# Reading the moving operand of every float32r product in a turned order: a linear-attention and gated feed-forward block on one core

## The chip, the cores and the metric

The kernel runs on one core of one Trainium2 chip. The metric is the device time of one execution in microseconds; lower is better. The five engines of the core that matter here are TensorE (PE in the profile; its weight loads are listed as PEld), VectorE (DVE), ScalarE (ACT), GpSimd (POOL), and SyncE (SP), whose queue issues all the DMAs.

## The reference

The input x has 2048 tokens of 512 features, all in float32. In short:

```python
xn = layernorm(x)                                   # over the features
q, k, v = split(xn @ wqkv)                          # 32 heads of 16
pq, pk = phi(q), phi(k)                             # phi(t) = (t + 1 if t > 0 else exp(t)) + 1e-6
kv = einsum("bhsd,bhse->bhde", pk, v);  z = pk summed over the tokens
o  = (pq @ kv) / (pq . z + 1e-6)
s  = o @ wo
g  = silu((gelu(xn @ w_gate) * (xn @ w_up)) @ w_down)   # inner width 1792
y  = x + s * g
```

The time of the kernel is mostly that of these matrix products.

## The kernel before, in words

**Products.** Accuracy is kept by splitting each float32 operand into a high and a low float32r part, and a product is made of three float32r matmuls: high by high, high by low, low by high (`three`, L443). The class `Sum` (L418) collects such parts into one PSUM bank; its inner function calls `nc.tensor.matmul(o, a, b)` (L437), where `o` is the output in PSUM, `a` the stationary operand (128 by 128, loaded as weights) and `b` the moving operand, 512 columns wide, and in the last two sums of the kernel 256. All float32r products of the kernel go through L437, but for two in `run_z` (L928). Plain float32 products are left in three places: the warming matmuls (L467), the transposes (L638), and the four small products for kv (L983); none of these is changed.

**Stages.** The program runs in one launch, in this order, with neighbours overlapped:

1. For 16 token tiles: layer norm, transposes, the products for q and k with a Strassen-like scheme of seven half-size products (banks named X, Y, Z, with the tokens as the stationary operand and the weights `kq` as the moving one), and phi. `gacc` adds up the Gram sums `gps` of the k features (moving: `pk`) over the tokens, and POOL adds up `zacc`. The transposed and split x tiles (`Xh`, `Xl`) are kept in SBUF, some are spilled to DRAM.
2. The feed-forward part, in two passes over the tokens (1024 each), each with seven pairs of 128-wide gate and up blocks. In `quad` (L1136), seven products per block go to the banks FX, FY and FZ; here the weights are stationary and x is moving, so the 512 columns of the output are tokens. The results leave PSUM through `esaved` (ACT copies into `fu`), `gelu` (ACT, straight from PSUM or from a sum), and `c_out` (DVE sums and products into `g` and `h`). From `h`, DVE and ACT make the split forms `hfh`, `hfl` (`h_form`, `h_sums`).
3. `down_strassen` (L1095) multiplies the forms of w_down (`dh`, `dl`, stationary) by `hfh`, `hfl` (moving) in the banks dX, dY, dZ and adds the results to the accumulators `acc` on DVE. It is interleaved with stage 2.
4. Attention's end: `pkv`, the matrix M made of it and wo, the normalised q transposed by tiles to DRAM (`turn`, L1218), and the sums `sps` (`attn`, L1260), M stationary and transposed q moving. `out_tile` (L1312) multiplies `sps` by the silu of `acc`, adds a tile of x transposed from DRAM (`sxr`) and writes the transposed output.

**Order.** The whole order of operations is written out in a list of 3626 numbers (`ORDER`, L18); each engine runs its own in that order, with semaphores between engines. So no engine takes work ahead of its turn.

**Host.** `kernel` (L1420) permutes some inputs before the launch: the q columns of wqkv and the features of x are laid out by heads (`order`), and x is given in transposed form too (`A_xT`). The output comes back transposed.

Of the kernel before, what the change touches and what calls it, by code (L numbers as in the profile page):

```python
# [10 lines left out]
AF = mybir.ActivationFunctionType  # L11
# [222 lines left out]
class Plan:  # L234
# [9 lines left out]
    def do(self, eng, cost, fn, out, *ins, more=(), lat=0.0, key=None, name="", kb=0, port=True, sum=None):  # L244


        op = Op()
        op.no, op.table, op.due = len(self.ops), TABLES.get(name), self.due
        op.eng, op.cost, op.lat, op.key, op.name = eng, cost, lat + self.HOP[eng], key, name
        op.fn = lambda: fn(out(), *[i() if isinstance(i, View) else i for i in ins])  # L250
        op.pre, op.suc, op.kb = set(), [], kb
        op.port = eng == "POOL" or eng == "DVE" and port and not any(
            isinstance(v, View) and v.psum for v in (out, *ins))
        outs = set(out.res)
        for m in more:
            outs.update(m.res)
        for i in ins:
            if isinstance(i, View):
                for r in i.res:
                    if r not in outs:  # L260
                        op.pre.update(r.writers)
                        r.readers.append(op)
        for r in outs:
            if sum is None or r.sum is not sum:
                r.before = {*r.writers, *r.readers}
                r.writers, r.readers, r.sum = [], [], sum
            op.pre.update(r.before)
            r.writers.append(op)
        for v in (out, *more, *ins):
            if isinstance(v, View) and v.gen:  # L270
                assert not v.gen.over, name
                if v.gen.prev:
                    op.pre.update(v.gen.prev.ops)
                v.gen.ops.add(op)

        op.banks = [v.gen for v in (out, *more, *ins) if isinstance(v, View) and v.psum and eng != "PE"]
        op.pre.discard(op)
        for p in op.pre:
            p.suc.append(op)
        self.ops.append(op)  # L280
        return op
# [5 lines left out]
def act(n, psum=False):  # L287
    return 0.06 + (0.00083 if psum else 0.00095) * n


def dve(n):
    return 0.065 + 0.00105 * n


def pool(n):
    return 0.18 + 0.0021 * n
# [3 lines left out]
def kernel(  # L300
# [14 lines left out]
    nc = tc.nc  # L315
# [6 lines left out]
    NC = 512  # L322
# [5 lines left out]
    do = plan.do  # L328
# [8 lines left out]
    def tile_in(pool_name, unit, shape, dtype, name, parts=1):  # L337

        gen = gens[pool_name, unit] = Gen(gens.get((pool_name, unit)))
        kept = []  # L340

        def get():
            if not kept:
                kept.append(pools[pool_name].tile(shape, dtype, name=name, tag=f"{pool_name}{unit}", bufs=1))
            return kept[0]
        v = View([Res() for _ in range(parts)], get, gen, pool_name == "ps")
        v.unit = unit
        return v
# [7 lines left out]
    def U(tag, places, name, dtype=F32, shape=(P, D), parts=1):  # L356
        return tile_in("up", ring(tag, places), list(shape), dtype, name, parts)
# [9 lines left out]
    def bank(i, name, shape=(P, D)):  # L367
        return tile_in("ps", i, list(shape), F32, name)
# [33 lines left out]
    def copy(eng, dst, src, n, name=""):  # L402
        if eng == "ACT":
            do("ACT", act(n, src.psum), lambda o, i: nc.scalar.copy(o, i), dst, src, name=name)  # L404
        else:
            do("DVE", dve(n), lambda o, i: nc.vector.tensor_copy(o, i), dst, src, name=name)

    def tt(eng, op, dst, a, b, n, name=""):
        e, c = (nc.vector, dve(n)) if eng == "DVE" else (nc.gpsimd, pool(n))
        do(eng, c, lambda o, p, q: getattr(e, f"tensor_{op}")(o, p, q), dst, a, b, name=name)  # L410
# [4 lines left out]

    subs = {}

    class Sum:  # L418


# [4 lines left out]
        def add(self, key, *parts, name="", cost=PASS):  # L425

            for n, part in enumerate(parts):
                regions = [abr[2] if len(abr) > 2 else None for abr in part]
                for r in regions:
                    self.passes[r] = self.passes.get(r, 0) + 1  # L430

                def run(o, *v, regions=regions):
                    for a, b, r in zip(v[::2], v[1::2], regions):

                        first = not self.on and not self.made
                        made = self.made[r] = self.made.get(r, 0) + 1
                        nc.tensor.matmul(o if r is None else o[:, r], a, b, start=first, stop=made == self.passes[r],  # L437
                                         skip_group_check=self.on or r is not None)
                do("PE", cost * len(part), run, self.ps, *[v for abr in part for v in abr[:2]],
                   key=(*key, "part", n), name=name, sum=self)  # L440
                subs.setdefault(key, []).append((*key, "part", n))
# [342 lines left out]
    for n in range(NP):  # L784
# [6 lines left out]
        for i in range(2):  # L791
# [6 lines left out]
            if n < CL:  # L798
                if i:
                    b = tile_in("up", 19 + n, [P, 2, 2, P], F32R, f"b12_{n}", 2)  # L800
# [113 lines left out]
    for c in range(KT):  # L914
        g = U("p", range(24, 28), f"GT{c}")
# [9 lines left out]

    def run_z(o, a, *zs):
        for n, z in enumerate(zs):
            nc.tensor.matmul(o, a, z, start=n == 0, stop=n == 1)  # L928
    do("PE", 2 * PASS, run_z, pz, ones_r, *zs, key="z")
    zq = const("zq", [P, P])  # L930

# [59 lines left out]
    for g in range(KT):  # L991
        v = tile_in("dp", 1 + g, [P, 2, D], F32R, f"wos{g}", 2)
        wos.append([v.part(v.res[hl:hl + 1], (slice(None), hl)) for hl in range(2)])
        split(*wos[g], wo_sb[g], D, "wo")
    for g in range(KT):
        pm = bank([6, 7, 5, 6][g], f"pm{g}")
        Sum(pm).add(("m", g), *three([[v[:, g] for v in kvs]], [wos[g]]), name="m")
        m = [tile_in("up", 19 + 2 * g + hl if g < 2 else 25 + 2 * g + hl, [P, D], F32R, f"m{hl}{g}") for hl in range(2)]
# [71 lines left out]
            for k in range(n):  # L1070
                ds[u, slots[k]] = [v[:, k] for v in f]

    def gelu(v, src, q, key):
        do("ACT", act(NC), lambda o, i: nc.scalar.activation(o, i, AF.Gelu_apprx_tanh), v, src, name="gelu")
        gs[key] = v

    hf, hforms = {}, {}
# [1 line left out]
    def h_form(u, slot, src):  # L1079
        f = hforms[u, slot] = U("hh", FHH, f"hfh{slot}_{u}", F32R), U("hl", FHL, f"hfl{slot}_{u}", F32R)  # L1080
        split(*f, src, NC, "h")

    def h_sums(p, u):
        def t():
            i = ring("hsum", range(3))
            return spare(p).part(spare(p).res[4 + i:5 + i], (slice(None), 2 + i))
        h = {key: hf.pop((u, key)) for key in (11, 12, 21, 22)}
        t1, t2, t3, t4 = t(), t(), t(), t()
        for slot, o, a, b in ((3, t1, h[12], h[11]), (4, t2, h[22], t1), (5, t3, h[22], h[12]), (6, t4, h[21], t2)):
            tt("DVE", "sub", o, a, b, NC, "T")  # L1090
            h_form(u, slot, o)
# [44 lines left out]
    def quad(q, p):  # L1136
        u, is_up = divmod(q % NQ, 2)

        def esaved(ps, name):
            e = U("fe", FE, name)  # L1140
            copy("ACT", e, ps, NC, name)
            return e

        def c_out(key, e, ps):

            if not is_up:
                g = U("fg", FG, f"g{key}_{q}")
                if e is None:
                    gelu(g, ps, q, (u, key))
                else:  # L1150
                    tt("DVE", "add", g, e, ps, NC, "c")
                    gelu(g, g, q, (u, key))
                return
            h = U("fc", [*FC, FX[0]], f"h{key}_{q}")
            g = gs.pop((u, key))
            if e is None:
                tt("DVE", "mul", h, g, ps, NC, "h")
            else:
                tt("DVE", "add", h, e, ps, NC, "c")
                do("POOL", pool(NC), lambda o, i: nc.gpsimd.tensor_mul(o, o, i), h, g, name="h")  # L1160
            hf[u, key] = h
            slot = {11: 0, 21: 1, 22: 2}.get(key)
            if slot is not None:
                h_form(u, slot, h)
            if key == 12:
                h_sums(p, u)

        X, Y, Z = bank(q % 2, f"FX{q}"), bank(2, f"FY{q}"), bank(3 + q % 2, f"FZ{q}")
        fprod(X, q, 1, True)
        copy("ACT", Y, X, NC, "seed")  # L1170
        fprod(Y, q, 2, False)
        c_out(11, None, Y)
        fprod(X, q, 6, False)
        u2 = esaved(X, f"fu2_{q}")
        fprod(Z, q, 5, True)
        fprod(X, q, 7, False)
        u3 = esaved(X, f"fu3_{q}")
        c_out(22, u3, Z)
        fprod(X, q, 4, False)
        c_out(21, None, X)  # L1180
        fprod(Z, q, 3, False)
        c_out(12, u2, Z)
# [204 lines left out]
    for c in range(2):  # L1387
        for n in range(KT):
            g = acc[1, 4 * c + n]
# [3 lines left out]
    for s in (0, 1, 4, 3, 5, 6, 2):  # L1393
        for hl in "hl":
            src = View([x_d[hl](j, ()).res[0] for j in range(4)], x_d[hl](0, (slice(None), slice(2 * s, 2 * s + 2))).get)
# [50 lines left out]
```

## Time and profile before

| What | Value |
|---|---|
| Time, median of 3 runs | 597.34 us (595.75 to 598.02) |
| Span of the profiled execution | 594.4 us; its time beside the span is not listed apart |
| TensorE busy, instructions | 586.5 us (99%), 2630 matmuls |
| VectorE busy | 485.8 us (82%), 774 |
| ScalarE busy | 360.1 us (61%), 668 |
| GpSimd busy | 242.7 us (41%), 237 |
| Moved by DMA | 141.29 MB, mean 238 GB/s |

In the rows that follow, a group is given as line, engine, operation, output and inputs by the program's names, partitions by elements, the count, and after the bar the busy time in us, the mean length of one in ns, and the idle time of that engine just before, with what ended it. Rows of a timeline begin with the start in us from the span's beginning and the length in us; where several like instructions follow each other they are merged, with their number at the end. A row of waits gives the waiting engine, the one waited for, and three numbers: us in total, times, longest. A matmul's record is longer than its share of the array, since matmuls overlap, so a rate is read from starts, not from lengths.

### The profile page before, as it was taken

The numbers are of one execution on the slowest core, as the hardware profiler recorded it, in microseconds if no ns is written. First come the engines' busy times: TensorE is split into PE (matmuls) and PEld (weight loads), VectorE is DVE, ScalarE is ACT, GpSimd is POOL, SyncE is SP. The second block draws the span as 40 slices with busy tenths as digits, with TensorE's granted clock in tenths as the row PEclk, the third lists the DMA queues.
The fourth block names the chain that finished last, engine by engine and source line by source line (L and its number), as shares of the span: only waits on it lengthen the run. The fifth ranks groups of instructions, "written<-read, shape, count | busy, mean of one in ns | idle before, by whom it ended". The sixth has DMA issues, their size and how long they took to land.

```text
span 594.4 us, 7882 instructions
## 1 busy us (share of the span) xinstructions
PE 586.5 (99%) x2630; PEld 485.4 (82%) x2630; DVE 485.8 (82%) x774; ACT 360.1 (61%) x668; POOL 242.7 (41%) x237
## 2 busy tenths in 40 slices
PE   9999999999999999999999999999999999999995
PEld 8888888888888888888888887888888888888875
DVE  7999988985887988899988764738787989788896
ACT  5788888877767856555446357856464436355810
POOL 4456776636646482734053822430302130126100
PEclk9999999999999999999999999999999999999998
DMA  7049987678864772736868989965575565638796
GB/s 252 32 146 289 281 254 227 203 254 312 311 219 179 261 290 82 291 133 236 298 252 263 366 322 351 370 254 178 182 243 175 189 239 177 212 124 283 242 288 249
DMA packets 78953, 141.29 MB, mean 238 GB/s; under 512 B 4673, under 2 KB 47681, under 8 KB 74945
## 3 DMA queue, kind: packets, MB, share of 16 engines
q1 hardware_dynamic: 78912, 140.79, 68.8%
q8 instruction: 21, 0.34, 0.2%
q14 instruction: 20, 0.16, 0.1%
HBM read 87.82 MB, written 52.95 MB: 237 GB/s over the span
## 4 chain that ended last, share of the span: by engine, by line
PE 93%; DMA 3%; DVE 2%; SPq 1%; issue 0%; DVEq 0%
PE FX L437 25%; PE FZ L437 13%; PE dX L437 12%; PE gps L437 7%; PE FY L437 6%; PE dY L437 6%; PE X L437 6%; PE sps L437 5%; PE dZ L437 3%; PE Z L437 3%; PE k L437 2%; PE q L437 2%; PE Y L437 1%; DMA Xl<-xl_d 1%; DMA sxr<-in_A_xT 1%; PE warm L467 1%
## 5 line engine op out<-in xcount | busy, mean ns | idle before, releaser
L437 PE MATMUL FX<-Xh,w 128*128 128x512 f32 x448 | 131.7, 390 | 0.0
L437 PEld LDWEIGHTS FX<-Xh,w 128*128 128x128 f32 x448 | 83.9, 188 | 17.7 <-ACT fu L404 0.4
L1160 POOL TENSOR_TENSOR h<-h,g 128x512 f32<-128x512 f32 x28 | 39.2, 1400 | 77.1 <-DVE h L410 39.7
L437 PE MATMUL FX<-Xl,w 128*128 128x512 f32 x224 | 68.3, 389 | 0.0
L437 PE MATMUL FZ<-Xh,w 128*128 128x512 f32 x224 | 68.2, 389 | 0.0
L410 POOL TENSOR_TENSOR sums<-draw 128x256 f32<-128x256 f32 x28 | 25.1, 897 | 96.1 <-DMA draw<-in_B_w_down 74.6
L404 ACT COPY dY<-dX 128x512 f32<-128x512 f32 x56 | 32.1, 574 | 48.6 <-PE dX L437 38.8
L404 ACT COPY fu<-FX 128x512 f32<-128x512 f32 x56 | 32.9, 588 | 47.2 <-PE FX L437 44.1
L437 PEld LDWEIGHTS FX<-Xl,w 128*128 128x128 f32 x224 | 42.0, 188 | 8.8
L437 PEld LDWEIGHTS FZ<-Xh,w 128*128 128x128 f32 x224 | 42.0, 188 | 8.7
L410 POOL TENSOR_TENSOR tmp<-raw 128x256 f32<-128x256 f32 x28 | 25.3, 907 | 48.5 <-DVE w L410 33.6
L1114 DVE TENSOR_TENSOR acc<-acc,dY 128x512 f32<-128x512 f32 x48 | 32.7, 682 | 15.1 <-PE dY L437 14.8
L1114 DVE TENSOR_TENSOR acc<-acc,dX 128x512 f32<-128x512 f32 x48 | 32.8, 683 | 14.1 <-PE dX L437 14.1
L437 PE MATMUL dX<-hfh,dh 128*128 128x512 f32 x112 | 43.4, 390 | 0.0
L404 ACT CAST hfh<-sums 128x512 fp32r<-128x512 f32 x56 | 34.2, 621 | 14.5 <-DVE sums L410 14.1
L437 PE MATMUL dX<-hfl,dh 128*128 128x512 f32 x112 | 42.6, 389 | 0.0
L437 PE MATMUL dX<-hfh,dl 128*128 128x512 f32 x112 | 42.4, 390 | 0.1
L410 DVE TENSOR_TENSOR hfl<-sums,hfh 128x512 fp32r<-128x512 f32 x56 | 40.0, 717 | 1.2 <-ACT hfh L404 0.9
L410 DVE TENSOR_TENSOR hfl<-h,hfh 128x512 fp32r<-128x512 f32 x42 | 32.7, 783 | 3.3 <-ACT hfh L404 2.3
L437 PE MATMUL FZ<-Xl,w 128*128 128x512 f32 x112 | 34.2, 391 | 0.6 <-DMA Xl<-xl_d 0.6
L437 PE MATMUL FY<-Xh,w 128*128 128x512 f32 x112 | 33.8, 389 | 0.0
L717 POOL TENSOR_TENSOR zacc<-zacc,kp 128x512 f32<-128x512 f32 x16 | 24.6, 1538 | 18.9 <-DVE kp L706 18.9
(222 smaller groups left out, 1513.1 us busy)
## 6 DMA issues: line engine op xcount, KB each, us to landing
w<-w_d SPq DMA_DIRECT2D x17, 1792.0 KB, 8.3
w_d<-w SPq DMA_DIRECT2D x11, 1792.0 KB, 7.4
draw<-in_B_w_down SPq DMA_DIRECT2D x14, 512.0 KB, 4.2
w_d<-we SPq DMA_DIRECT2D x18, 256.0 KB, 2.5
x<-in_A_x SPq DMA_DIRECT2D x16, 256.0 KB, 3.1
q_d<-qp SPq DMA_DIRECT2D x16, 256.0 KB, 3.1
qz<-q_d SPq DMA_DIRECT2D x16, 256.0 KB, 4.2
q<-q_d SPq DMA_DIRECT2D x16, 256.0 KB, 3.0
```

Of the source, the lines that this page charges most:

```text
L404: do("ACT", act(n, src.psum), lambda o, i: nc.scalar.copy(o, i), dst, src, name=name)
L410: do(eng, c, lambda o, p, q: getattr(e, f"tensor_{op}")(o, p, q), dst, a, b, name=name)
L437: nc.tensor.matmul(o if r is None else o[:, r], a, b, start=first, stop=made == self.passes[r], skip_group_check=self.on or r is not None)
L467: nc.tensor.matmul(o, w, w, start=True, stop=True)
L717: do("POOL", pool(D), lambda o, i: nc.gpsimd.tensor_add(o, o, i), zacc, p0, name="zacc")
L1114: do("DVE", dve(D), lambda o, i: nc.vector.tensor_add(o, o, i), o, ps, name="acc")
L1160: do("POOL", pool(NC), lambda o, i: nc.gpsimd.tensor_mul(o, o, i), h, g, name="h")
```

## The change

Each float32r product reads its moving operand's columns in a turned order. In every eight columns 0 to 7 the order is 0, 4, 1, 5, 2, 6, 3, 7, so that a read alternates between the first four and the last four. The output's columns come out in that order. The stationary operand, the widths, the number of products, `ORDER` and the DMAs stay.

The rest of the change undoes or carries that order:

- In stage 1 the columns are features of q and k; the columns of wqkv are permuted on the host with the inverse (for k twice, since k's features pass through a second turned product in `gacc` and in the z product). wo is permuted by the inverse once.
- In stage 2 the columns are tokens. `esaved`, `gelu` and `c_out` read PSUM through a view that steps (0, 2, 4, 6, 1, 3, 5, 7 in each eight) and so write SBUF in the natural order.
- In stages 3 and 4 the tokens come out turned once on both sides (`acc` and `sps`); x transposed is turned on the host to match, and the host turns the output back.

```diff
+    def turned(ap):
+        return ap.rearrange("p (o i m) -> p o m i", i=2, m=4)
+    def back(v):
+        return v.map(lambda ap: ap.rearrange("p (o m i) -> p o i m", i=2, m=4))
+    def eights(v):
+        return v.map(lambda ap: ap.rearrange("p (o i m) -> p o i m", i=2, m=4))
...
-                        nc.tensor.matmul(o if r is None else o[:, r], a, b, start=first, stop=made == self.passes[r],
+                        nc.tensor.matmul(o if r is None else o[:, r], a, turned(b), start=first, stop=made == self.passes[r],
...
-            nc.tensor.matmul(o, a, z, start=n == 0, stop=n == 1)
+            nc.tensor.matmul(o, a, turned(z), start=n == 0, stop=n == 1)
...
-    def gelu(v, src, q, key):
-        do("ACT", act(NC), lambda o, i: nc.scalar.activation(o, i, AF.Gelu_apprx_tanh), v, src, name="gelu")
+    def gelu(v, src, q, key, to=None):
+        do("ACT", act(NC), lambda o, i: nc.scalar.activation(o, i, AF.Gelu_apprx_tanh), to or v, src, name="gelu")
...
-            copy("ACT", e, ps, NC, name)
+            copy("ACT", eights(e), back(ps), NC, name)
...
-                    gelu(g, ps, q, (u, key))
+                    gelu(g, back(ps), q, (u, key), eights(g))
...
-                    tt("DVE", "add", g, e, ps, NC, "c")
+                    tt("DVE", "add", eights(g), eights(e), back(ps), NC, "c")
...
-                tt("DVE", "mul", h, g, ps, NC, "h")
+                tt("DVE", "mul", eights(h), eights(g), back(ps), NC, "h")
...
-                tt("DVE", "add", h, e, ps, NC, "c")
+                tt("DVE", "add", eights(h), eights(e), back(ps), NC, "c")
...
+    eights = _np.arange(8).reshape(2, 4).T.ravel()
+    def turned(n):
+        return (_np.arange(0, n, 8)[:, None] + eights).ravel()
+    def back(n):
+        return _np.argsort(turned(n))
-    laid["A_xT"] = _np.ascontiguousarray(laid["A_x"].T)
+    laid["A_xT"] = _np.ascontiguousarray(laid["A_x"].T[:, turned(shape[-2])])
...
-    laid["A_wqkv"] = _np.concatenate([w[:, :d][:, order], w[:, d:2 * d], w[order, 2 * d:]], 1)
+    laid["A_wqkv"] = _np.concatenate([w[:, :d][:, order[back(d)]], w[:, d:2 * d][:, back(d)[back(d)]], w[order, 2 * d:]], 1)
+    laid["A_wo"] = _np.ascontiguousarray(laid["A_wo"][:, back(d)])
...
-    return _np.ascontiguousarray(r.results[0]["out_yT"].T).reshape(shape)
+    return _np.ascontiguousarray(r.results[0]["out_yT"].T[back(shape[-2])]).reshape(shape)
```

## The prediction

> **What bounds the kernel now.** I read the page's busy times first, then the granted clock, the waits of TensorE, the chain that ended last, the starts of single products, and last the busy time by stretches.
>
> ```profile
> span 594.4 us, 7882 instructions
> PE 586.5 (99%) x2630; PEld 485.4 (82%) x2630; DVE 485.8 (82%) x774; ACT 360.1 (61%) x668; POOL 242.7 (41%) x237
> PE 93%; DMA 3%; DVE 2%; SPq 1%; issue 0%; DVEq 0%
> ```
> ```profile
> core 0: 594.4 us, clock 0.997
> ```
> ```profile
> PE warm L467 <- DVE neg_half L459: 1.1, 1, 1.1
> PE FZ L437 <- DMA Xl<-xl_d: 0.6, 1, 0.6
> ```
>
> TensorE is busy for 99% of the span, waits 1.7 us in all for others, and makes 93% of the chain. Its clock is granted nearly in full, so the throttle holds nothing back. The time is therefore the number of products times the time from one start to the next. The busy column can't give that (a product's record is 390 ns long and overlaps the next), so I take starts:
>
> ```profile
> 299.74 0.39 PE L437 MATMUL dY<-hfl,dh 128*128 128x512 f32 x1
> ...
> 303.82 0.39 PE L437 MATMUL dZ<-hfh,dh 128*128 128x512 f32 x1
> ```
> ```profile
> 586.67 0.64 PE L437 MATMUL sps<-pqh,Ml 128*128 128x256 f32 x4
> 587.15 1.12 PE L437 MATMUL sps<-pqh,Mh 128*128 128x256 f32 x8
> ```
> ```profile
> 144.23 2.84 PE L983 MATMUL pkv<-GT,wvo 128*128 128x128 f32 x24
> 146.83 0.70 PE L437 MATMUL FX<-Xh,w 128*128 128x512 f32 x2
> ```
>
> Between the first two rows 18 products of 512 columns start: 4.08 us / 18 = 226.7 ns each. Four products of 256 columns take 0.48 us, 120 ns each. The difference, 106.7 ns for 256 columns, is 0.417 ns a column. Take 512 of those (213.4) from 226.7 and **13.3 ns are left that belong to the product, whatever its width**. The columns themselves already stream at an even rate; the only thing that a better order of reading can win is this remainder, 32 column times per product.
>
> The third pair is the plain float32 product, on the same array and with its own load of weights: 2.60 us / 24 = 108.3 ns for 128 columns. At two column times a column that is 106.7 ns, and 1.6 ns remain. So a load of weights between products doesn't by itself cost 13.3 ns; the remainder goes with float32r, which takes its moving columns twice as fast.
>
> **The change part by part.** *The products.* All float32r products read turned. Their number is the page's 2630 less the plain float32 ones:
>
> ```profile
> L638 PE MATMUL pt<-blk,xn 128*128 128x128 f32 x48 | 7.5, 284 | 0.0
> L467 PE MATMUL warm<-blk 128*128 128x128 f32 x28 | 6.1, 407 | 1.1 <-DVE neg_half L459 1.1
> L983 PE MATMUL pkv<-GT,wvo 128*128 128x128 f32 x32 | 3.9, 275 | 0.0
> L437 PEld LDWEIGHTS FX<-Xh,w 128*128 128x128 f32 x448 | 83.9, 188 | 17.7 <-ACT fu L404 0.4
> ```
>
> 2630 - 48 - 28 - 32 = 2522, and 2522 x 13.3 ns = 33.5 us of remainder in the whole span. No row of this trace has a turned read, so its price has to be bounded. Best end: the remainder goes altogether, -33.5 us. Worst end: a column costs two column times, as in the plain float32 rows, some +0.213 us a product. What I take is a remainder of 1.6 ns, that of the plain float32 row: 11.7 ns x 2522 = **-29.5 us on TensorE**. My reason is what the 32 column times look like. They are the same for 256 and 512 columns, so they follow something that each product has once, and the load of 128 weight columns (188 ns, under way while the product before it streams) is that. Plain float32 has the load too but takes a moving column only every second tick, and pays nearly nothing. So the moving read and the weight read seem to meet when the moving read runs at full rate, one lost tick for four weights. [...] This is a choice between two readings of one number, not a row.
>
> [...]
>
> *The un-turning where TensorE's results leave PSUM in the feed-forward part* (esaved, gelu, the sums and products of c_out). The same instructions, as many elements; PSUM is now read every second column, and SBUF is written in order.
>
> ```profile
> L404 ACT COPY fu<-FX 128x512 f32<-128x512 f32 x56 | 32.9, 588 | 47.2 <-PE FX L437 44.1 <-DVE g L410 2.9
> L410 DVE TENSOR_TENSOR h<-fu,FZ 128x512 f32<-128x512 f32 x28 | 19.1, 682 | 11.1 <-PE FZ L437 10.8 <-ACT fu L404 0.2
> L410 DVE TENSOR_TENSOR g<-fu,FZ 128x512 f32<-128x512 f32 x28 | 19.0, 680 | 9.4 <-PE FZ L437 8.3 <-DMA s_d<-so 1.2
> L1074 ACT ACTIVATE g<-FY 128x512 f32<-128x512 f32 x14 | 8.4, 599 | 1.4 <-PE FY L437 1.4
> L1074 ACT ACTIVATE g<-FX 128x512 f32<-128x512 f32 x14 | 8.3, 596 | 5.4 <-PE FX L437 5.3
> L410 DVE TENSOR_TENSOR h<-g,FX 128x512 f32<-128x512 f32 x14 | 9.5, 680 | 5.5 <-PE FX L437 5.5
> L410 DVE TENSOR_TENSOR h<-g,FY 128x512 f32<-128x512 f32 x14 | 9.5, 678 | 1.0 <-PE FY L437 1.0
> L404 ACT CAST xnh<-xn 128x512 fp32r<-128x512 f32 x16 | 9.9, 624 | 0.9 <-PE gps L437 0.8
> L404 ACT CAST hfh<-h 128x512 fp32r<-128x512 f32 x42 | 25.9, 621 | 6.1 <-POOL h L1160 3.4 <-PE dY L437 2.7
> L612 DVE STREAM_TRANSPOSE sums<-q 128x512 f32<-128x512 f32 x16 | 17.5, 1093 | 0.2
> ```
> ```profile
> L404 ACT COPY fu<-FX x56: 578/587/599, 140.3 to 535.7; 128x512 f32<-128x512 f32 x56
> ```
>
> That is 84 instructions on ACT (56 + 14 + 14) and 84 on DVE (28 + 28 + 14 + 14). Lower end: nothing, as the cast through a permuted view (xnh, runs of 32, most of its 16) takes 624 ns beside 621 in order; a shorter read would end off TensorE's path and gain nothing there. Upper end: the transpose, whose writes step by four elements, 1093 ns, so +0.41 us on each DVE one. I take nothing: xnh is a plain pass with a view, as these are, while the transpose is another operation. The cover is the idle time that the rows show: both engines wait for TensorE before these very instructions (44.1, 10.8, 8.3 us). Were the cover gone at the upper end, the 84 on DVE would add 34.5 us to it over 395 us (140.3 to 535.7), 4.4 us in each 50.
>
> *Layout.* Weights, x transposed and the output are permuted on the host; the same DMAs move the same bytes. The z product's turned read undoes the columns of k. Nothing is added to a queue.
>
> *What is late next.* If TensorE wants 5% less (29.5 of 594.4), the others must keep up in the same order.
>
> ```profile
> 20.00:60.00 40.00, 40.00 (x186) 33.07 (x185) 36.48 (x64) 30.29 (x55) 22.25 (x21) 1.00 0.57 166
> 60.00:100.00 40.00, 40.00 (x185) 32.85 (x184) 36.08 (x65) 32.86 (x62) 28.07 (x26) 1.00 0.83 255
> 250.00:300.00 50.00, 50.00 (x223) 41.39 (x222) 46.37 (x76) 26.67 (x53) 13.32 (x13) 1.00 0.68 239
> 350.00:400.00 50.00, 49.43 (x217) 40.41 (x217) 26.40 (x40) 33.66 (x58) 16.69 (x16) 1.00 0.87 320
> ```
>
> The columns after the length are busy PE, weight loads, DVE, ACT, POOL, then clock, DMA share and GB/s. DVE has 46.37 of 50 in the third row; 50 less 5% is 47.5, so it fits with 1.1 us of air. In the first two it has 72.6 of 80, against 76. In the fourth the x tiles come back from DRAM with the DMA engines at 0.87, and TensorE's one wait for data, 0.6 us, is there. I count the gain of that stretch as lost (50 us x 5% = 2.5), half of the other three's (130 us x 5% / 2 = 3.2), 5.7 in all: an estimate, from those shares.
>
> *The sum:* 594.4 - 29.5 + 5.7 = 570.6 us of span. The median of the three runs, 597.34, is 2.9 above the profiled span, which I keep: **573.5 us**, 4% faster. If nothing is given back and the whole remainder goes, 564; if half the remainder goes, 597.3 - 16.8 + 3 = 584.
>
> **The rivals.** *The order doesn't touch the remainder.* If the 32 column times are a gap between one product's last column and the next one's first, every product keeps 226.7 ns. For it: being independent of the width. Against it: the plain float32 rows, which change weights as often and have 1.6. Time: 597.
>
> *The turned read is slower.* The place is the moving read of every float32r product: in order, four columns lie side by side before the read moves 16 bytes on; turned, every read lands in the other group of four than the last. If the array then takes two column times a column, as it does in the plain float32 rows, 2522 products add up to 0.213 us each, +537: about 1130 us. It decides early: 3 us / 2522 is 1.2 ns a product, three lost column times in 512. Against it stands only that in order the move to the next group, every fourth column, costs nothing that the slope of 0.417 ns shows. [...]
>
> *DVE takes over.* TensorE gets its 29.5 us, but the stepped reads of PSUM cost the 0.41 us above. DVE then needs 46.37 + 4.4 = 50.8 us for what is now the stretch 250 to 300, more than TensorE needs today, and 4.4 more in each of its neighbours. What is left is the gain ahead of 140 us, 140 x 5% = 7 us, and little after it: about 590. For it: DVE is the next engine. Against it: the 624 beside 621.
>
> **How the numbers follow.** About 0.5% (3 us) is what a measurement can tell from no change; the three runs lie within 2.3 us. Chances: remainder mostly or half gone 0.60 (564 to 585); DVE takes over 0.07 (585 to 596, by its size faster for 0.05 and the same for 0.02); order without effect 0.13 (595 to 599); turned read slower 0.20. Hence faster 0.65, same 0.15, slower 0.20. The slow case, with a tail to 1130, is what I leave out: the range is 563 to 600. The likeliest case alone has 564 to 585.
>
> **What the changed profile would show.** Starts of 512 columns 213 to 218 ns apart and of 256 some 108: the step on the products is right; both still 13 ns above the columns: the first rival; a difference of the two above 107 ns: the second. The fu, g and h rows at 588, 597 and 680 ns: the un-turning is free; DVE rows near a microsecond and waits of TensorE for DVE: the third. What is given back shows as waits of TensorE, for DMA near 350 to 400 first. Wrong altogether would make me a granted clock below 0.99, which this trace gives no reason to expect.

## The result, and the profile after

The changed kernel takes 572.08 us (median of 4 runs, 571.42 to 573.22) against 597.1 before: ratio 0.958, 95% interval 0.956 to 0.960. The forecast was 573.5. Its profiled execution took 573.22 us, 1.8 more than its span. From that page and from the answers on clock and waits of the changed kernel:

```profile
span 571.4 us, 7894 instructions
PE 559.5 (98%) x2630; PEld 486.3 (85%) x2630; DVE 486.6 (85%) x774; ACT 358.6 (63%) x668; POOL 242.7 (42%) x237
PE 86%; DMA 5%; DVE 4%; issue 2%; POOL 1%; SPq 0%; ACT 0%; DVEq 0%; POOLq 0%
```
```profile
PE FZ L448 <- DMA Xl<-xl_d: 2.4, 1, 2.4
...
PE dX L448 <- DVE acc L1125: 0.8, 1, 0.8
...
```

The same 2630 matmuls, still bound by TensorE, but no longer by it alone: its share of the chain falls from 93 to 86%, and its waits grow from 1.7 to 4.7 us (beside those shown, the 1.1 at the start as before and two of 0.2, one of them for x from DRAM). The starts of products, from the timeline of the changed kernel:

```profile
279.65 0.59 PE L448 MATMUL FX<-Xl,w 128*128 128x512 f32 x2
...
283.96 0.38 PE L448 MATMUL dX<-hfh,dl 128*128 128x512 f32 x1
```
```profile
562.86 0.61 PE L448 MATMUL sps<-pqh,Ml 128*128 128x256 f32 x4
563.30 1.06 PE L448 MATMUL sps<-pqh,Mh 128*128 128x256 f32 x8
```

Twenty products start in 4.31 us, 215.5 ns each (the long stretch of the first bench below gives 215.8), and those of 256 columns stand 110 ns apart. By the bench's figure 10.9 ns of 226.7 are gone, and 2.4 ns remain beside the 213.4 of the columns. The groups that un-turn:

```profile
L404 ACT COPY fu<-FX 128x512 f32<-128x512 f32 x56 | 32.8, 586 | 39.7 <-PE FX L448 35.4 <-DVE g L410 3.9
L410 DVE TENSOR_TENSOR h<-fu,FZ 128x512 f32<-128x512 f32 x28 | 19.0, 679 | 9.5 <-PE FZ L448 8.9 <-ACT fu L404 0.4
L1085 ACT ACTIVATE g<-FY 128x512 f32<-128x512 f32 x14 | 8.4, 599 | 1.1 <-PE FY L448 1.1
```

586, 679 and 599 ns against 588, 682 and 599: the stepped reads of PSUM cost nothing that these rows show; what shrinks is the wait for TensorE ahead of them.

### The profile page after: what moved, and what is told of

Read it like the earlier page. It is cut to its first block, busy times and chain, and to the rows that moved or that the text cites. A ratio compares the mean times of both kernels' runs of the same rounds, so it can differ in the third digit from the quotient of the medians.

```text
span 571.4 us, 7894 instructions
## 1 busy us (share of the span) xinstructions
PE 559.5 (98%) x2630; PEld 486.3 (85%) x2630; DVE 486.6 (85%) x774; ACT 358.6 (63%) x668; POOL 242.7 (42%) x237
## 4 chain that ended last, share of the span: by engine, by line
PE 86%; DMA 5%; DVE 4%; issue 2%; POOL 1%; SPq 0%; ACT 0%; DVEq 0%; POOLq 0%
PE FX L448 23%; PE FZ L448 12%; PE dX L448 11%; PE gps L448 7%; PE FY L448 6%; PE X L448 5%; PE dY L448 5%; PE dZ L448 3%; PE Z L448 3%; PE sps L448 2%; DMA sxr<-in_A_xT 2%; PE k L448 2%; PE q L448 2%; DMA Xl<-xl_d 2%; DMA g<-g_d 1%
## 5 line engine op out<-in xcount | busy, mean ns | idle before, releaser
L448 PE MATMUL FX<-Xh,w 128*128 128x512 f32 x448 | 127.0, 380 | 0.0
L448 PE MATMUL FX<-Xl,w 128*128 128x512 f32 x224 | 66.1, 379 | 0.2 <-DMA Xl<-xl_d 0.2
L448 PE MATMUL FZ<-Xh,w 128*128 128x512 f32 x224 | 65.9, 379 | 0.0
L448 PE MATMUL FZ<-Xl,w 128*128 128x512 f32 x112 | 33.0, 381 | 2.4 <-DMA Xl<-xl_d 2.4
L966 POOL TENSOR_TENSOR qz<-qz,zq 128x512 f32<-128x512 f32 x16 | 21.7, 1355 | 22.4 <-DMA qz<-q_d 18.5
```

The costliest lines, as they stand in the source:

```text
L448: nc.tensor.matmul(o if r is None else o[:, r], a, turned(b), start=first, stop=made == self.passes[r], skip_group_check=self.on or r is n ...
L966: do("POOL", pool(D), lambda o, z: nc.gpsimd.tensor_mul(o, o, z.unsqueeze(1).to_broadcast([P, KT, P])), rows_of(q), zq, name="u")
```

## The experiments

**Which part of the change does it.** Two kernels split it in two.

`turn_only`, the changed kernel without the un-turning:

```diff
     def back(v):
-        return v.map(lambda ap: ap.rearrange("p (o m i) -> p o i m", i=2, m=4))
+        return v
     def eights(v):
-        return v.map(lambda ap: ap.rearrange("p (o i m) -> p o i m", i=2, m=4))
+        return v
```

> The change without the un-turning in the feed-forward part: all products read turned, but esaved, gelu and c_out read PSUM in order (the feed-forward part's tokens are then in another order than the attention part's, which the kernel does not mend). If the stepped PSUM reads are free, as predicted: within 0.3% of the changed kernel, 571 to 574 us, and the fu, g and h rows at 587, 679, 596 ns in both. If they cost something that the rows hide, such as a later release of a bank: 1 to 3 us less than 572.

Measured: 571.45 us, ratio to before 0.959 (0.957 to 0.961), which overlaps with the changed kernel's.

`unturn_only`, the changed kernel with products in order:

```diff
-  nc.tensor.matmul(o if r is None else o[:, r], a, turned(b), ...
+  nc.tensor.matmul(o if r is None else o[:, r], a, b, ...
...
-  nc.tensor.matmul(o, a, turned(z), start=n == 0, stop=n == 1)
+  nc.tensor.matmul(o, a, z, start=n == 0, stop=n == 1)
```

> The un-turning without the turned products: every product reads in order, esaved, gelu and c_out keep their stepped reads (so the columns are un-turned that were never turned). Theory A and B alike: the whole gain sits in the products, so this runs as the kernel before, 595 to 599 us with starts 226.7 ns apart. If the stepped reads themselves helped or hurt: away from 597 by over 3 us.

Measured: 596.53 us, ratio 1.000 (0.999 to 1.002). The whole gain sits in the order of reading, and the un-turning costs nothing that can be told from noise (the fu, h and g rows of `turn_only`, which reads PSUM in order, have 585, 680 and 599 ns, those of the changed kernel 586, 679 and 599).

**Which orders are fast.** A bench of bare products, one order per stretch of 40.

> Nothing of the block is computed: 16 stretches of 40 products each (128 weight columns, 512 moving columns, back to back, 16 different weight tiles in turn), one order of reading per stretch; read are the starts of the products. Theory A (the moving read at full rate meets the reading of the weights, and an order that alternates between two groups of four columns, 16 bytes each, has room to give way): in order 226.7 ns, turned 215.8, groups of four swapped but read in order (swapped) 226.7, alternating inside a group of four (infour) 226.7, alternating between groups 32 bytes, 64 bytes and 1 KB apart (insixteen, inthirtytwo, infar) 216, four groups in turn (fourlines) 216; bf16 in order 216, since it reads half the bytes. Theory B (the 13 ns are a gap between two products that the turned order happens to shorten, with nothing to do with weights): same for the alternating orders, but bf16 and float32r in order should then differ by no rule, and loading one and the same weight tile every time (oneweight) changes nothing. Theory C (every change of 16-byte group costs): turned would be dearer than in order, which the run of the whole kernel already contradicts; it can still hold for orders that never come back to a group soon (everysecond, everyline: a new group at each of 512 reads): over 226.7, up to 427 ns, where theory A has them at 216 too.

The timeline of this bench; each row is a stretch, and the next start less this one, divided by 40, is the time of one product:

```profile
26.50 9.43 PE L53 MATMUL inorder<-mv,w 128*128 128x512 f32 x40
35.76 8.79 PE L53 MATMUL turned<-mv,w 128*128 128x512 f32 x40
44.39 17.43 PE L53 MATMUL everysecond<-mv,w 128*128 128x512 f32 x40
61.65 9.46 PE L53 MATMUL swapped<-mv,w 128*128 128x512 f32 x40
70.94 13.74 PE L53 MATMUL steptwo<-mv,w 128*128 128x512 f32 x40
84.51 9.45 PE L53 MATMUL infour<-mv,w 128*128 128x512 f32 x40
93.80 8.79 PE L53 MATMUL insixteen<-mv,w 128*128 128x512 f32 x40
102.43 8.80 PE L53 MATMUL inthirtytwo<-mv,w 128*128 128x512 f32 x40
111.06 8.80 PE L53 MATMUL infar<-mv,w 128*128 128x512 f32 x40
119.69 10.90 PE L53 MATMUL fourlines<-mv,w 128*128 128x512 f32 x40
130.43 18.63 PE L53 MATMUL everyline<-mv,w 128*128 128x512 f32 x40
148.88 8.83 PE L53 MATMUL bfloat<-mvb,wb 128*128 128x512 bf16 x40
```

In order 231.5, turned 215.8, alternating 32 bytes, 64 bytes or 1 KB apart (insixteen, inthirtytwo, infar) 215.8 as well. Alternating inside a group of four columns (infour) 232: no gain. Four groups in turn (fourlines) 268, where I had 216; steptwo (0, 2, 4, 6, 1, 3, 5, 7) 339; a new group at each read 431 and 461. So alternating is not what helps by itself, and the orders tried here that leave a group after one column are far dearer (268 to 461). Theory A had 216 for a new group at each read too. The stretch `swapped` is no order of its own: as it is written it reads in order from column four on, and its 232 say no more than that.

In order is 231.5 here and not 226.7. The likely reason is where the four moving tiles lie: in the last bench, with tiles 4096 bytes apart, in order takes 226.8, and in this one, with a single moving tile for all products (`onemoving`, not shown), 227.0. No run varies the addresses alone.

**Whether the weights are to blame.** The prediction's reason was that the moving read collides with the reading of the next product's weights (theory A), an estimate from the 32 column times beside 128 weight columns.

> Nothing of the block is computed: stretches of 40 products, in order and turned, with fewer weight columns, fewer moving columns, and weights spread apart in SBUF. Theory A: what a product costs beside its columns grows with the weights read for it: 128 columns 13.3 ns, 64 columns (halfin) about 7.9, 32 (quarterin) about 5.2, so starts 221 and 218.5 ns apart; turned 215.8 at every width. Narrower moving tiles keep the 13.3: 256 columns 120 ns in order and 109 turned, 128 columns about 67 in order and 56 turned unless the load itself is then the limit. Weights in every second column (bytwo) and every fourth (spreadin): if the collisions count 16-byte groups, the remainder goes to about 24 and 46 ns (237 and 259 ns apart); if they count weights, it stays at 13.3. Theory B (a gap between products): halfin and quarterin stay at 226.7, and the spread weights too. Starting the moving tile two columns off a group of four (shifted) should leave in order at 226.7 by both; turned then crosses groups unevenly and may land between 215.8 and 226.7 by theory A.

The weight loads and the timeline of that bench:

```profile
L53 PEld LDWEIGHTS halfin<-mv,w x40: 134/134/136, 44.4 to 53.4; 128*64 128x64 f32 x40
L53 PEld LDWEIGHTS quarterin<-mv,w x40: 107/108/109, 62.3 to 71.2; 128*32 128x32 f32 x40
```
```profile
44.66 9.36 PE L53 MATMUL halfin<-mv,w 128*64 128x512 f32 x40
53.86 8.80 PE L53 MATMUL halfturned<-mv,w 128*64 128x512 f32 x40
62.49 9.32 PE L53 MATMUL quarterin<-mv,w 128*32 128x512 f32 x40
71.65 8.79 PE L53 MATMUL quarterturned<-mv,w 128*32 128x512 f32 x40
80.28 4.87 PE L53 MATMUL narrowin<-mv,w 128*128 128x256 f32 x40
```

With half the weights a product in order takes 230 ns, with a quarter 229, while the load falls from 188 ns to 134 and 108. Theory A had 221 and 218.5. It falls: the loss doesn't count the weights. One weight tile loaded again and again (`oneweight` of the first bench, not shown) leaves a product at 236.5 ns, no less than the 231.5 of that bench. Turned stays at 215.8 with half and with a quarter of them. Theory B, a gap between two products, had half and quarter unchanged and is not refuted here, but it has no account of why the order should decide.

Three other pairs of this bench are not shown. Weights spread to every fourth column take 240.5 ns in order and 233 turned, but there a load takes 309 to 328 ns, longer than the time from start to start, so this pair may be held by the loads, which no row shows, and says little of the moving read. With the moving tile two columns off a group of four, in order takes 235, where 226.7 was expected, and turned 231.5, so turned loses most of its gain there. Products of only 128 columns take 110.5 ns in order and 111.5 turned, where theory A had 67 and 56: turned products of 256 columns take 111.5 too, so half the columns bring nothing more. 110 to 112 ns is the floor of the float32r stretches in these benches, all with 128 weight columns at these widths; what sets it no run shows.

**A rule for the orders.** What the first bench leaves is theory D, the author's own reading of its times. It goes by the order alone: the columns at its even places are taken as one stream and those at its odd places as another, and what counts is how many reads in a row of a stream lie in one group of four float32r columns (16 bytes). With four in both streams a product took 215.8 ns in that bench (turned, insixteen, inthirtytwo, infar), with two 231.5 and 232 (in order, infour), with one 268 to 461 (fourlines, steptwo, everysecond, everyline). That the array fetches in two streams, as the theory has it, is an estimate from these times; no run shows how the array fetches.

> Nothing of the block is computed: stretches of 40 products, other orders, all tiles at starts of like alignment in SBUF. Theory A (collision with the weights) has fallen in the runs on widths: a quarter of the weights still cost 229 ns in order. Theory D: the columns at even and at odd places of the order are fetched as two streams; a stream keeps full rate when four of its reads in a row lie in one group of 16 bytes, loses 5 to 7% with two, and half or more with one. By D: in order 227 to 232 (two per group in each stream); turned 215.8 also when it starts four columns later, but 227 or more when it starts one column off; each column read twice in a row (doubled: 0,0,1,1,2,2,3,3) 216; pairs read twice (doubledpairs: 0,1,0,1) 216; every second float32r column (stepped: one per group and stream) 340 to 460; bf16 in order 216 (four per stream); every second bf16 column (bfloatstepped: two per stream) 227 to 232; the same turned between two groups (bfloatturned: four per stream) 216. Theory E (float32r is dearer since it needs four bytes a column, and alternating between two groups helps): bfloatstepped and bfloatturned both 216, doubled no better than in order. Width: if the loss is per column, in order 512, 384 and 256 columns lose in proportion (11, 8, 5.5 ns beyond a floor); if per product, 11 each.

```profile
75.28 8.79 PE L55 MATMUL turnedofffour<-mv,w 128*128 128x512 f32 x40
83.92 10.96 PE L55 MATMUL turnedoffone<-mv,w 128*128 128x512 f32 x40
94.71 8.80 PE L55 MATMUL doubled<-mv,w 128*128 128x512 f32 x40
103.34 8.80 PE L55 MATMUL doubledpairs<-mv,w 128*128 128x512 f32 x40
111.98 18.30 PE L55 MATMUL stepped<-mv,w 128*128 128x512 f32 x40
130.10 8.83 PE L55 MATMUL bfloat<-mvb,wb 128*128 128x512 bf16 x39
138.76 9.20 PE L55 MATMUL bfloatstepped<-mvb,wb 128*128 128x512 bf16 x39
147.80 21.87 PE L55 MATMUL bfloatturned<-mvb,wb 128*128 128x512 bf16 x40
168.99 9.88 PE L55 MATMUL last<-mv,w 128*128 128x512 f32 x40
```

The float32r stretches go by D: turned four columns later 216, one column off 270, doubled 216, doubled pairs 216, stepped 453. So does the tile two columns off in the bench before, which leaves each stream two in a row. For bf16 (40 products a stretch, one record missing in two) in order is 216.5 and every second column 226, as D had it and E had not; but bfloatturned takes 530 ns, where both had 216. So D is no rule for stepped bf16 reads; why is open. And its "half or more" for one read in a row is too dear for fourlines of the first bench, 268 ns, where a stream comes back to a group after one other. That can't be the whole reason, since steptwo does so too and takes 339.

The direct test moves one stream against the other:

```diff
+    v = ap.rearrange("p (o i m) -> p o m i", i=2, m=4)
+    steps = [list(s) for s in v.ap]
+    steps[-1][0] = b          # the odd places read b columns behind the even ones; turned is b = 4
```

> Nothing of the block is computed: stretches of 40 products, with all moving tiles at starts of 4096 bytes. First question, per product or per column: in order at 512, 448, 384, 320 and 256 columns beside turned at the same widths. The prediction had 13.3 ns per product at any width; the earlier bench, at other starts, had 14.1, 12.4 and 9.1 ns over turned or its floor for 512, 384, 256. If per column: the loss over turned falls with the width, to half at 256; if per product, it stays. Second, theory D (even and odd places of the order are two streams, each wanting four reads in a row from one group of 16 bytes): the odd places are shifted against the even ones, which keep four per group. Shifted by eight columns (lageight): four per group in both, 215.8. By two or by six (lagtwo, lagsix): two and two in the odd stream, 220 to 232. By one (lagone): three and one, 230 to 270. If instead only the number of groups touched by eight reads counts: lagtwo (groups 0 and 1, as turned) is 215.8, lagsix (groups 0, 1, 2) dearer. Third: a quarter of the weights in order, if the weights have no part at all the same as infull; 229 against 232 before.

```profile
29.44 9.23 PE L60 MATMUL infull<-mv,w 128*128 128x512 f32 x40
38.51 8.27 PE L60 MATMUL infoureight<-mv,w 128*128 128x448 f32 x40
46.61 7.12 PE L60 MATMUL inthreeeight<-mv,w 128*128 128x384 f32 x40
53.57 6.02 PE L60 MATMUL inthreetwenty<-mv,w 128*128 128x320 f32 x40
59.43 4.96 PE L60 MATMUL intwofifty<-mv,w 128*128 128x256 f32 x40
64.22 8.80 PE L60 MATMUL turnfull<-mv,w 128*128 128x512 f32 x40
72.86 7.73 PE L60 MATMUL turnfoureight<-mv,w 128*128 128x448 f32 x40
80.43 5.60 PE L60 MATMUL turnthreetwenty<-mv,w 128*128 128x320 f32 x40
85.86 4.63 PE L60 MATMUL turntwofifty<-mv,w 128*128 128x256 f32 x40
90.33 10.83 PE L60 MATMUL lagone<-mv,w 128*128 128x512 f32 x40
100.99 9.24 PE L60 MATMUL lagtwo<-mv,w 128*128 128x512 f32 x40
110.06 9.23 PE L60 MATMUL lagsix<-mv,w 128*128 128x512 f32 x40
119.12 8.80 PE L60 MATMUL lageight<-mv,w 128*128 128x512 f32 x40
127.76 9.44 PE L60 MATMUL quarterin<-mv,w 128*32 128x512 f32 x40
137.04 9.25 PE L60 MATMUL last<-mv,w 128*128 128x512 f32 x40
```

Shifted by eight 216, by two 226.8 and by six 226.5, by one 266.5. Two columns of shift touch the same two groups per eight reads as turned does and still lose 11 ns: the count of groups is not the rule; four in a row for each stream fits. Here the even places kept four in a row and the odd ones alone lost them, and the loss is that of a plain read, in which both have two. On the width: in order less turned is 10.8 ns at 512 columns (226.8 less 216), 13.3 at 448 (202.5 less 189.2) and 10.8 at 320 (146.5 less 135.8). At 256 it is 119.8 against 111.8, but there turned stands on the floor of 110 to 112, so the 8 are a lower bound. The loss belongs to the product rather than to its columns. A quarter of the weights gives 232, no less than all.

**The rule in the whole kernel.** `in_fours` reads 0, 2, 1, 3 in each four (in `turned`, m=2 for m=4) on top of `turn_only`.

> The whole kernel with every float32r product reading 0, 2, 1, 3 in each four columns, and nothing un-turned (the output's columns stay in that order and the two parts of the block don't match in it). Theory D: each stream still has two columns per group of 16 bytes, so starts stay at 226.7 ns and the time at 595 to 599 us, although the order is as unusual for the array as the turned one. Theory E, if what helps is that neighbours in the order are not neighbours in SBUF: 572.

Measured: 596.69 us, ratio 1.000 (0.9985 to 1.0014). An unusual order that leaves two reads in a row to each stream gains nothing.

**Where 27 us of products became 25 of time.** The longest new wait is for a reloaded low x tile near 343 us, whose load stands in SyncE's queue behind a load of w_down. Five reloads were put ahead of it:

```diff
-        return [self.ops[n] for n in ORDER]
+        early = [2331, 2329, 2335, 2333, 2334]     # reloads of x
+        o = [n for n in ORDER if n not in early]
+        i = o.index(2455) + 1                      # a load of w
+        return [self.ops[n] for n in o[:i] + early + o[i:]]
```

> The changed kernel with four reloads of the low x tiles and one of the high placed ahead of a load of w_down and of two stores in SyncE's queue. The changed kernel's longest wait of TensorE, 2.4 us for such a tile near 343 us, has the reload issued at 335 to 339 us behind that load, though what it overwrites is read for the last time at 329. If the queue's order makes it late: the wait goes, 569.5 to 571 us against 572.1. If the DMA engines are simply full there (0.94 of the stretch 300 to 350): the tiles land no sooner together, the wait moves to another tile and the time stays within 0.2% of 572.

Measured: 577.48 us, ratio to before 0.968 (0.966 to 0.969) where the changed kernel has 0.958: some 5 us worse. The waits of TensorE, and its timeline after the longest:

```profile
PE dX L451 <- ACT dY L407: 4.2, 1, 4.2
```
```profile
350.35 2.77 PE L451 MATMUL FX<-Xh,w 128*128 128x512 f32 x6
352.91 0.64 PE L451 MATMUL FX<-Xl,w 128*128 128x512 f32 x2
```

The wait for x is gone and a longer one has come: the load of w_down, now behind the reloads, lands at 345.2 us, POOL's sums wait 10.9 us for it, ScalarE's queue stands 6.7 us behind those sums, and TensorE waits 4.2 us for a copy in that queue. After it six products take 2.56 us, 427 ns each; the mean granted clock of the whole execution is 0.991, where the changed kernel has 0.998. (After the changed kernel's wait of 2.4 us six such products start in 1.29 us, 215 ns each, and the granted clock is 1.00 from 345 to 355 us.) The two together explain the loss between the two traces: 1.8 us more of waiting and 11 products at 211 ns more, 2.3 us, beside spans of 575.3 and 571.4.

`early_x_tail` is `early_x` with five of the last ten stores issued by ScalarE.

> As early_x, and five of the last ten stores of the output are issued from ScalarE's queue instead of SyncE's. In the changed kernel SyncE issues the last seven stores one after another from 563.8 to 567.9 us, while VectorE is done at 566.0. With two queues the last store can be issued at about 566.2 and land some 2.5 to 3 us later: 1.5 to 2 us off the end, 568 to 569.5 us if early_x keeps its part. If the landing and not the issue holds up the end: no difference from early_x.

Measured: 578.06 us (576.07 to 578.97), not distinguishable from `early_x` (577.14 to 577.91). The last stores are issued by 571.7 us, 4.6 before the end of the span; in the changed kernel, with one queue, by 567.9, 3.5 before it. A second queue for issuing the stores doesn't shorten the end here.

`two_early` moves only 2331 and 2329, and `two_first` moves them ahead of 2455 too; `after_again` is the changed kernel beside them.

> As early_x, but only the two low x tiles that TensorE waited for in the changed kernel are moved ahead of the load of w_down (behind the load of w in the queue). In early_x all five moved reloads were in front of that load of w_down, which landed at 345.2 us instead of 340.9 and held up POOL, then ScalarE, then TensorE by 4.2 us. Two tiles are 1 MB of the five's 2.5 MB: if the order among the transfers decides, the load of w_down lands some 1.7 us later than in the changed kernel and is just in time; TensorE's 2.4 us wait goes, 569.5 to 571 us against 572. If the engines are so full (0.93 to 1.0 from 320 to 346 us) that any order leaves somebody late: 572 to 574.

> As two_early, with the two tiles also ahead of the 1.8 MB load of w in SyncE's queue. If what is late at 343 us is only a matter of which transfer goes first: the load of w lands about 3 us later; it is used from about 341 us on, so this ends between 569.5 us (it has the slack) and 574 us (TensorE waits for w instead of x).

> The changed kernel once more, beside the two others on the same chip, so that differences of less than half a per cent can be read: 571 to 573 us, with TensorE's wait for a low x tile near 343 us at 2 to 3 us.

Measured: 571.88, 572.73 and 571.93 us, all within a quarter of a per cent. Two rows, of the waits of `two_first` and of `after_again`:

```profile
PE FX L451 <- DMA w<-w_d: 1.9, 1, 1.9
```
```profile
PE FZ L448 <- DMA Xl<-xl_d: 0.7, 1, 0.7
```

In `two_first` another tile is late instead of x, and in this second execution of the changed kernel the wait for x is 0.7 us where it was 2.4. In `two_early` TensorE waits for no transfer any more, and the time is still the same; where the 0.7 us went is not shown. The DMA engines are full there (0.94 of the stretch 300 to 350 in the first trace of the changed kernel), and no order of these loads that was tried gains anything. None of the versions beats the changed kernel.

## Why the prediction was right

*The remainder.* 13.3 ns a product beside the columns, whatever the width, was the base of the sum. The last bench bears it out: what the order wins stays with the product down to 320 columns, and at 256 as far as the floor lets it be seen.

*The term.* 11.7 ns x 2522 = 29.5 us was forecast from plain float32's remainder of 1.6 ns. Measured are 10.8 ns x 2522 = 27.2. So the remainder is the term that was a little off: 2.4 ns and not 1.6. The plain row is in doubt as a source for it: its products of 128 columns come every 108.3 ns, and float32r products of 128 columns, with half the time for their columns, come no faster than every 110.5. The plain row may be held by the same floor and say nothing of the read; no run tests it. The bench's bf16 stretch (216.5 ns, 3.1 beside the columns) comes near the 2.4.

*The reason given was wrong.* The choice of the good end rested on a collision with the weight loads, and that a turned read would escape it no row showed. The benches refute it as far as it counts weights: with a quarter of them a product in order still takes 229 and 232 ns. What fits every float32r order tried is how many reads in a row the even and the odd places of the order each have from one group of 16 bytes: with four a product takes 215.8 to 216 ns, with two 226.5 to 235, with three and one 266 to 270, with one 268 to 461. The number came out because the choice between the ends was right, not its argument; that this order has four in a row for each stream is, as far as the argument goes, luck. Why two in a row cost some 11 ns per product (10.8 at 512 and at 320 columns, 13.3 at 448) is still open.

*The un-turning at nothing* was right, to about 0.1% by `turn_only` (571.45 us against 572.08).

*What is given back.* 5.7 us were forecast, half of it to DMA around 350 and half to VectorE in three stretches. Measured are 27.2 less the 23.0 that the two spans differ by, 4.2 us: 3.0 more of waiting, and 8.1 us from the start of the last group of products to the end (571.4 less 563.3) for 7.2 before (594.4 less 587.15); why the end is longer was not looked into. Of the waits 2.6 are for x from DRAM, at the place foreseen; VectorE gives 0.8, at the end and not in the three stretches, so that part was too dear. The two misses, 2.3 us too much gain and 1.5 too much given back, nearly cancel, and that is luck. How much is given back also depends on the execution: the trace of `after_again` has a span of 569.7, 24.7 below that before, and so gives back 2.5. The step from span to time was off too: 2.9 us were added, a median less the span of another execution, where the same execution has 1.8.

*The rivals.* "The order doesn't touch the remainder" is out, though its premise, a loss that goes by product, is borne out. "The turned read is slower" did not happen in this order, but its price is real for others: everyline takes 461 ns, where two column times a column were worked out as 440. Turned goes to another group of 16 bytes at every read too, and takes 215.8. "DVE takes over" needed dear PSUM reads, which there are not (679 ns in the h row beside 682).

## What to carry to other kernels

Where float32r products run back to back, measure the time from start to start at two widths, both well above the shortest time that narrow products reach (110 to 112 ns here). What it has beside the columns can depend on the order of reading: 13.3 ns for a product in order fell to 2.4 when even and odd places of the order each had four reads in a row from one 16-byte group. All float32r orders tried with that property did so (0, 4, 1, 5 ..., or with 32 bytes or a kilobyte between the two: 215.8 to 216 ns), but a tile that started one or two columns off a group lost it (270 and 231.5). For bf16 read at a step it failed: 530 ns with four in a row. Where such an order must be undone, a stepped PSUM read in the instruction that empties the bank was free here (586 and 679 ns beside 588 and 682), and host layout took care of the rest.

## What the runs showed of the hardware that was not expected

In `early_x` a wait of TensorE of 4.2 us was followed by products at 427 ns, half the rate, for some 4 us; after the changed kernel's wait of 2.4 us they came every 215 ns. A turned read that starts one column off its group was dearer (270 ns) than any read in order (226.7 to 235). And a turned read of stepped bf16 columns took 530 ns, more than two column times a column (427 ns).
